# Moving the deferred token tiles' share of the last evacuations of a spectral block into its inverse stage

## The chip, the cores and the metric

One NeuronCore of a Trainium2 chip runs the kernel. The metric is the device time of one execution in microseconds; lower is better. Before the change it is 485.93 (median of three runs, 485.89 to 487.13).

The engines' names: PE is TensorE (matrix products; PEld is its weight load), DVE is VectorE, ACT is ScalarE, POOL is GpSimd and SP is SyncE. Of these SP and POOL issue the transfers (DMA). Products are written to PSUM, eight banks, used here in four pairs; ACT and DVE copy ("evacuate") them to SBUF.

## The reference

The input `x` has 2048 tokens of 576 features. A spectral filter is added to it, and then a gated feed-forward network.

```python
def _A_ref(x, w_r, w_i):
    X = rfft2(x.astype(float32), axes=(-2, -1))
    X = X * (w_r + 1j * w_i)
    return irfft2(X, s=(S, D), axes=(-2, -1)).astype(bfloat16)

def _B_ref(x, w_gate, w_up, w_down):
    return (gelu(x @ w_gate) * (x @ w_up)) @ w_down

h = x + _A_ref(layernorm(x), w_r, w_i)
h2 = h + _B_ref(layernorm(h), w_gate, w_up, w_down)
```

## The kernel before

The Fourier transforms are products with constant tables. The 2048 tokens stand as 16 tiles of 128 (tile c holds every sixteenth token). There are five parts in time:

1. Layer norm and the first transform over the tokens (to about 20 us), in the order of the list `SEQ1`.
2. The spectral stages over 16 groups of frequencies (20 to 43 us), in the order of the list `SEQF`. `D`/`d` and `B` finish the forward transform, `T` multiplies by the filter, `V`/`v` begin the way back, `R`/`r` do so for the 32 remainder columns that do not fit into 256, four groups at a time. Capital and small letter are the two halves of one accumulation on PE; behind the small one stand its evacuations.
3. The inverse stage (43 to 55 us), in the order of the list `SEQ`, for token tiles 0 to 7. `I`/`i` (function `i_mm`, line 837) are the products over groups, `E` their evacuation to GS, `N`/`o` (`n_mm`, line 854) the products with the inverse table IT, `a` (line 860) adds the result to x on DVE; then `s`, `q`, `c`, `n`, `u`, `e` normalise the tile and transpose it. `G0` and `G1` are the first products of the network.
4. The network's products with the gate and up weights (line 946), and among them the inverse stage of token tiles 8 to 15, which are *deferred* (`def_i`, line 996, and `def_n`, line 1013).
5. The products with the down weights (line 1046 and 1058) and the output, by blocks of 512 tokens.

The order on each engine is that of the lists: each engine runs its instructions in the order in which the program issues them. A recorder (`Prog`) turns reads and writes of named tiles into semaphore waits. An instruction that must wait for more than a few semaphores is preceded by wait instructions of their own, issued at line 307.

What the change touches:

- `st_V` writes group i's result to the tile V, `[128, 2, 2, 16 token tiles, 16 groups, 2, 4]`, in one or two evacuations (line 608, in `ev`). For the last one, V15, ACT and DVE take 256 elements per partition each. All token tiles are in them.
- `st_R` handles the remainder. For its first three sets (R0 to R2) one evacuation goes to the buffer RB, and eight transfers of 8 KB carry it to the places in VR. They are split by `k = (2 * j + t_) % 3 > 0`: three on SP, five on POOL. For the last set, R3, eight evacuations of 32 partitions by 128 elements go to VR directly, four on ACT and four on DVE.
- `i_mm(c, False)` makes four products from V (*main* products); `i_mm(c, True)` makes four more and then two from VR. VR is read with the token tile as its innermost index.
- `LOADS` says behind which step the transfers of tables and of the first weights are issued on SP. `"r0": "t"` calls `tab_load` behind r0: it waits for the last copy of the filter, and issues the tables VT (parts 2 to 5), DT, IT and IDT. The pieces a0 to a5 and b0 to b5 are the network's first weights (256 and 896 columns wide); each waits until PE has come to the step by which it is named.
- `SLOT` gives each `I`, `N` and `u` a pair of PSUM banks: the free one that was used longest ago. R3 has pair 3 (banks 6 and 7) and V15 pair 2 (banks 4 and 5). In `SEQ`, I0, I1 and I2 take pairs 0, 1 and 2, and N0 pair 3.

Of the kernel before, what the change touches and what calls it, by code (L numbers as in the profile page):

```python
# [12 lines left out]
NZ, NY = 5, 3  # L13
# [16 lines left out]
DENG, BENG = ['act', 'dve', 'act', 'act', 'act', 'act', 'act', 'act', 'dve', 'act', 'act', 'act', 'act', 'act', 'act', 'act'], ['act', 'dve', 'act', 'act', 'act', 'act', 'act', 'dve', 'act', 'act', 'act', 'act', 'act', 'act', 'act', 'act']  # L30
LOADS = {"r0": "t", ".I0": "a0 a1 a2 a3 a4 a5", ".N0": "b0", ".i3": "b1", ".o1": "b2", ".N3": "b3", ".o3": "b4 b5", ".i7": "d"}
RENG = ['dve', 'act', 'act', 'act', 'act']
QR = ((0, 1), (1, 2), (2, 3), (3, 4), (4, 8), (8, 16))
DEF0, DSTEP = 3, 4
SEQ = """I0 I1 I2 i0 E0S i1 E1S i2 E2A N0 I3 o0 i3 N1 I4 o1 a0 E3S N2 o2 a1 s0A q0 i4 a2 s1A I7 c0 N3 E4S q1 s2D i7 I6 o3 E7A i6 c1 N4 o4 a3 q2 E6A c2 N7 I5 o7 a4 n0P N6 s3A a7 i5 n1P n2P q3 c3 o6 u1 U1 u2 E5A u0 U2 a6 n3P e1A e2D U0 N5 u3 e0A o5 a5 U3 G0 e3D G1""".split()

# [10 lines left out]
def build_tables():  # L47
# [106 lines left out]
    assert np.allclose(VN[0, 0], VN[0, 1])  # L154
    T["VTAB"] = np.stack([v if k else v.reshape(128, 4, 16, 4).transpose(0, 1, 3, 2).reshape(128, 256) for v, k in ((VN[0, 0], 1), (VN[0, 0], 0), (VN[1, 0], 1), (VN[1, 1], 1), (VN[1, 0], 0), (VN[1, 1], 0))], 1).reshape(128, -1)

# [175 lines left out]
def _build(nc, A_x, A_w_r, A_w_i, B_w_gate, B_w_up, B_w_down, out):  # L332
# [78 lines left out]
    TR = sb.alloc("TR", [128, 2, 2, 2, 128], BF16)  # L411
    RB = sb.alloc("RB", [128, 3, 2, 2, 4, NT], BF16)

# [18 lines left out]
    P.op(POOL, lambda g: g.memset(EXQ[:, :], -0.5), w=["EXQ"])  # L432
    P.op(POOL, lambda g: g.memset(VR[:, :, :, :, :], 0.0), w=[("V", g, 2 + t) for g in range(NG) for t in range(2)])
    xv = A_x[0].rearrange("(p c) d -> p c d", c=NT)
# [243 lines left out]
    def st_V(i, second, engs):  # L678
        g, z, b0 = GORD[i], i % NZ, FB["V", i]

        def mm(h, o, ct, first, last, after):
            c, t_ = ct
            return P.op(PE, lambda t: t.matmul(bank(b0 + o, 0, 128, 128 * c, 128 * c + 128), TP[64 * h:64 * h + 64, z, o, t_, c:256:2], VT[64 * h:64 * h + 64, 0 if g else 2 + o, t_, :],  # L683
                                               start=first, stop=last), r=[("T", z), "VT" if g else "VT2"], w=[("PS", b0 + o)], after=after)

        halves(("V", i), second, [[(c, t_) for c in range(2) for t_ in range(2)]] * 2, mm)
        if not second:
            return
        v5 = V[:, :, :, :, g, :, :].rearrange("p c t n j e -> p j (c t n) e")
        n = 2 // len(engs)  # L690
        for a, e in enumerate(engs):
            ev(e, v5[:, n * a:n * a + n], banks(b0 + a, n, 256).rearrange("p a (c e) -> p a c e", e=4), [("PS", b0 + a + k) for k in range(n)], [("V", g, a + k) for k in range(n)])

    def st_R(q, second):
        js = range(4 * q, 4 * q + 4)
        b0 = FB["R", q]

        def mm(h, o, pt, first, last, after):
            part, t_ = pt
            return P.op(PE, lambda t: t.matmul(bank(b0 + o, 0, 128, 128 * part, 128 * part + 128), TR[64 * h:64 * h + 64, q % 2, o, t_, :], VT[64 * h:64 * h + 64, 4 + o if part else 1, t_, :], start=first, stop=last),  # L700
                        r=[("TR", q % 2, j) for j in range(4)] + ["VT2" if part else "VT1"], w=[("PS", b0 + o)], after=after)

        halves(("R", q), second, [[(part, t_) for part in range(1 + (q == 3)) for t_ in range(2)]] * 2, mm)
        if not second:
            return
        keys = [("PS", b0), ("PS", b0 + 1)]
        if q < 3:
            ev(RENG[q], RB[:, q, :, :, :, :].rearrange("p t o e n -> p o t (e n)"), banks(b0, 2, 128).rearrange("p o (t x) -> p o t x", t=2), keys, [("RB", q)])
            for j, i in enumerate(js):
                for t_ in range(2):  # L710
                    k = (2 * j + t_) % 3 > 0
                    P.dma((SP, POOL)[k], VR[64 * t_ + 32 * (j % 2):64 * t_ + 32 * (j % 2) + 32, GORD[i], :, :, :], RB[32 * j:32 * j + 32, q, t_, :, :, :], f"r{q}{k:d}", r=[("RB", q)], w=[("V", GORD[i], 2 + t_)])
            return
        for i in js:
            j, g = i % 4, GORD[i]
            for t_ in range(2):
                dst = VR[64 * t_ + 32 * (j % 2):64 * t_ + 32 * (j % 2) + 32, g, :, :, :].rearrange("p o e n -> p o (e n)")
                src = PS[32 * j:32 * j + 32, b0 * 512:(b0 + 2) * 512].rearrange("p (a c) -> p a c", a=2)[:, :, 128 * (i == LAST) + 64 * t_:128 * (i == LAST) + 64 * t_ + 64]
                ev((ACT, DVE, DVE, ACT)[j], dst, src, keys, [("V", g, 2 + t_)])

# [35 lines left out]
    def tab_load():  # L756
        P.op(SP, None, after=[last])
        P.dma(SP, VT[:, 2:6, :, :].rearrange("p a b c -> p (a b c)"), dram["VTAB"][:, 512:1536], "vt2", w=["VT2"])
        P.dma(SP, DT[:, :, :].rearrange("p a b -> p (a b)"), dram["DTAB"][:, :], "dt", w=["DT"])
        P.dma(SP, IT[:, :, :, :].rearrange("p a b c -> p (a b c)"), dram["ITAB"][:, :], "it", w=["IT"])  # L760
        P.dma(SP, IDT[:, :], dram["EYE"][:, :], "eye", w=["IDT"])

# [14 lines left out]
    def loads(w):  # L777
        for v in LOADS.get(w, "").split():
            if v in "td":
                (tab_load if v == "t" else tab2_load)()  # L780
            else:
                wg0_part(int(v[1]), *((0, 256, ["WGA"]) if v[0] == "a" else (256, 1152, [("WG", 0, i) for i in range(4)])))
# [24 lines left out]
    vk = [vmain, vmain, vtail]  # L807
    vkeys = vmain + vtail


    SLOT, last, held, ing = {}, [sorted(used.values()).index(used[2 * b]) - 4 for b in range(4)], set(), False
    for t, w in enumerate(SEQ):
# [18 lines left out]
    def i_mm(c, second):  # L831
        b, e = SLOT["I", c], ends.setdefault(("I", c), [None, None])
        for j in range(2 + second):
            for r in range(2):
                o, r0 = r ^ (not second), 64 * r
                lhs = V[r0:r0 + 64, j, o, c, :, :, :] if j < 2 else VR[r0:r0 + 64, :, :, :, c].rearrange("p g o e -> p (g o e)")
                e[o] = P.op(PE, lambda t, r0=r0, o=o, j=j, lhs=lhs: t.matmul(bank(b + o, 0, 128, 0, KW), lhs, DT[r0:r0 + 64, 2 * o + j if j < 2 else 4, 0:KW], start=(not second and j == 0), stop=(second and j == 2)),  # L837
                            r=vk[j] + ["DT"], w=[("PS", b + o)], after=[e[o]] if second and j == 0 else [])
# [119 lines left out]
    def gu_first(i):  # L958
        for a in range(4):
# [4 lines left out]
           "s": lambda c, e: sq(c, ENG[e]), "q": ln2_q, "c": ln2_c, "n": lambda c, e: norm(c, ENG[e]), "u": lambda c: turn_mm(c, False), "U": lambda c: turn_mm(c, True),  # L964
           "e": turn_ev, "G": gu_first}
    for w in SEQ:
# [16 lines left out]

    fdead = ["DT", "IT", "J0", "J1", "ZD"] + [(n_, c) for n_ in ("ATB", "ATS") for c in range(NT)] + [("G", i // 2, i % 2) for i in range(10)] + [*[("Y", a) for a in range(NY)], *[("RB", a) for a in range(3)]]
    fdead += [("T", a) for a in range(NZ)] + [("TR", a, j) for a in range(2) for j in range(4)]
# [3 lines left out]
    def def_i(c, second):  # L989
        e = ends.setdefault(("X", c), [None, None])  # L990
        for j in range(3):
            for r in range(2):
                o, r0 = r ^ (not second), 64 * r
                t_ = j if j < 2 else r
                lhs, rhs = (V[r0:r0 + 64, o, t_, c, :, :, :], DP[r0:r0 + 64, 2 * o + t_, :]) if j < 2 else (VR[r0:r0 + 64, :, :, :, c].rearrange("p g o e -> p (g o e)"), DP[r0:r0 + 64, 4 + o, :])
                e[o] = P.op(PE, lambda t, o=o, t_=t_, lhs=lhs, rhs=rhs, j=j: t.matmul(bank(6 + o, 0, 128, HK * t_, HK * t_ + HK), lhs, rhs, start=(not second and j == 0), stop=(second and j == 2)),  # L996
                            r=vk[o if j < 2 else 2] + ["DP"], w=[("PS", 6 + o)], after=[e[o]] if second and j == 0 else [])
        if not second:
# [133 lines left out]
```

## Time and profile before

| what | value |
|---|---|
| median of the runs | 485.93 us (485.89, 485.93, 487.13) |
| the profiled execution's own time | 485.97 us |
| its span in the trace | 484.2 us |
| granted TensorE clock | 1.00 |
| L946 (gate and up), products of one shape | 2142 + 486, 373 to 376 ns each |
| L1046 (down) | 2160, 283 ns each |
| L837 + L854 (inverse stage), share of the last chain | 0.7% + 0.2% |

The span is what the trace covers; the time of an execution has 1.8 us around it. PE has 99% of the span as busy time, since products overlap and each counts from its start to its modelled end, so the share does not tell where it waits. For that one reads the chain of work that ended last and the timeline. A line of the timeline has the start, the length, the engine and source line, the operation, the tiles written and read, the shape and the number of instructions merged; in brackets stands the engine's idle time before them and who ended it. "SPq" lines are issues of transfers, and their length is that of the issue, not of the transfer.

### The profile page before, as it was taken

To read this page: it belongs to the slowest core of one execution; us is meant where nothing else is said; L and a number is where in the kernel's file an instruction comes from. 1 tells how busy PE (TensorE), PEld (TensorE's weight loads), DVE (VectorE), ACT (ScalarE), POOL (GpSimd) and SP (SyncE) were. 2 spreads that over 40 slices of the span, in tenths; PEclk is the share of its full clock that TensorE was granted. 3 is DMA by queue.
4 is the path that set the end of the run, shared out by engine and by line. 5 is a ranking of instruction groups with operands and counts; after the bars stand their busy time and mean duration, and the time that the engine had idled before them with its cause. 6 is when DMAs were issued, how large, how long until landed. Compare 5 with 4: busy or idle time off the path is not lost.

```text
span 484.2 us, 12895 instructions
## 1 busy us (share of the span) xinstructions
PE 477.5 (99%) x5875; PEld 304.4 (63%) x5876; DVE 183.3 (38%) x366; ACT 146.3 (30%) x295; POOL 52.2 (11%) x88
## 2 busy tenths in 40 slices
PE   8999999999999999999999999999999999999998
PEld 4877765555588744444688644444788544445884
DVE  7898755665500144333200234333101233333011
ACT  6998753434300032233100132223100133223000
POOL 6873317010120000000000000000000000000000
DMA  8865889941430001000000011000000000000000
GB/s 283 215 142 160 251 279 282 374 109 27 173 100 27 26 15 23 20 1 0 3 14 15 26 24 23 13 1 1 3 14 27 14 1 1 0 1 1 3 26 26
DMA packets 28582, 33.19 MB, mean 69 GB/s; under 512 B 12640, under 2 KB 21872, under 8 KB 28528
## 3 DMA queue, kind: packets, MB, share of 16 engines
q1 hardware_dynamic: 24864, 19.87, 14.3%
q0 software_dynamic: 3664, 12.50, 8.1%
q8 instruction: 46, 0.75, 0.7%
q14 instruction: 8, 0.07, 0.1%
HBM read 26.21 MB, written 2.36 MB: 59 GB/s over the span
## 4 chain that ended last, share of the span: by engine, by line
PE 95%; DMA 1%; DVE 1%; POOL 1%; SPq 0%; issue 0%; POOLq 0%; DVEq 0%
PE PS L946 58%; PE PS L1046 27%; PE PS L642 2%; PE PS L1058 2%; PE PS L683 2%; DMA XO<-in_A_x_dram 1%; PE PS L553 1%; PE PS L662 1%; PE PS L837 1%; PE PS L996 1%; DVE XO L860 1%; SPq L242 0%; PE PS L1013 0%; PE PS L854 0%; POOL XN L569 0%
## 5 line engine op out<-in xcount | busy, mean ns | idle before, releaser
L946 PE MATMUL PS<-HT,WG 64*128 64x512 bf16 (+1 forms) x2142 | 233.5, 373 | 0.1
L946 PEld LDWEIGHTS PS<-HT,WG 64*128 64x128 bf16 x2142 | 116.1, 94 | 104.4 <-DVE AT L955 0.2
L954 ACT ACTIVATE GL<-PS 128x512 bf16<-128x512 f32 x144 | 85.7, 596 | 281.7 <-PE PS L946 281.7
L955 DVE TENSOR_TENSOR AT<-GL,PS 128x512 bf16<-128x512 bf16 x144 | 98.8, 687 | 166.0 <-ACT GL L954 166.0
L1046 PE MATMUL PS<-WD,AT 64*128 64x288 bf16 x2160 | 133.0, 283 | 0.0
L1046 PEld LDWEIGHTS PS<-WD,AT 64*128 64x128 bf16 x2160 | 114.3, 94 | 18.7
L1033 DVE TENSOR_TENSOR OS<-PS,XO 128x288 bf16<-128x288 f32 (+2 forms) x32 | 13.2, 452 | 125.5 <-PE PS L1046 118.0
L946 PE MATMUL PS<-HT,WGX 64*128 64x512 bf16 x486 | 53.5, 376 | 0.0
L946 PEld LDWEIGHTS PS<-HT,WGX 64*128 64x128 bf16 x486 | 25.7, 94 | 26.7
L863 ACT ACTIVATE OS<-XO,NM 128x576 bf16<-128x576 bf16 x15 | 11.6, 773 | 11.4 <-DVE XO L1017 11.4
L642 PE MATMUL PS<-FT,U 64*128 64x288 bf16 x160 | 13.3, 283 | 0.0
L675 DVE TENSOR_TENSOR TP<-YS,WS 128x1024 bf16<-128x1024 bf16 x16 | 11.0, 686 | 0.4 <-PE PS L683 0.2
L564 ACT ACTIVATE U<-PS 128x384 bf16<-128x384 f32 (+2 forms) x31 | 10.5, 427 | 1.2 <-PE PS L553 1.1
L496 DVE BATCH_NORM_STATS2 ST<-XO 128x6 f32<-128x288 bf16 x26 | 10.0, 441 | 1.8 <-DMA XO<-in_A_x_dram 1.8
L242 POOL DMA_DIRECT2D WG<-in_B_w_gate_dram x9 | 6.1, 679 | 35.5 <-DMA WG<-in_B_w_gate_dram 32.1
L683 PE MATMUL PS<-VT,TP 64*128 64x128 bf16 x256 | 9.9, 217 | 0.0
L553 PE MATMUL PS<-ATS,XO 128*128 128x128 bf16 x96 | 8.2, 220 | 1.5 <-POOL ATS L522 0.8
L242 POOL DMA_DIRECT2D WD<-in_B_w_down_dram x9 | 6.7, 756 | 22.9 <-PE PS L1013 22.9
L608 ACT ACTIVATE CUS<-PS 128x576 bf16<-128x576 f32 x14 | 9.1, 656 | 0.4 <-PE PS L642 0.2
L1058 PE MATMUL PS<-WD,AT 128*128 128x448 bf16 (+1 forms) x72 | 9.0, 286 | 0.0
L538 PE MATMUL PS<-ZD 128*128 128x512 bf16 x23 | 7.5, 484 | 1.5 <-POOL ZD L431 1.5
L608 ACT ACTIVATE YS<-PS 128x576 bf16<-128x576 f32 x14 | 8.8, 653 | 0.1
(88 smaller groups left out, 231.3 us busy)
## 6 DMA issues: line engine op xcount, KB each, us to landing
WD<-in_B_w_down_dram POOLq DMA_DIRECT2D x9, 576.0 KB, 13.0
WG<-in_B_w_up_dram SPq DMA_DIRECT2D x6, 576.0 KB, 6.6
WG<-in_B_w_gate_dram POOLq DMA_DIRECT2D x6, 576.0 KB, 6.2
out_dram<-OS SPq DMA_DIRECT2D x30, 72.0 KB, 1.7
XO<-in_A_x_dram SPq DMA_DIRECT2D x3, 576.0 KB, 7.1
WGX<-in_B_w_up_dram SPq DMA_DIRECT2D x2, 576.0 KB, 4.5
WGX<-in_B_w_gate_dram POOLq DMA_DIRECT2D x2, 576.0 KB, 5.8
HT<-HN SPq DMA_TRANSPOSE x60, 2.4
```

The source lines that it names most:

```text
L242: fn = lambda e: e.dma_start(out_ap, in_ap)
L553: P.op(PE, lambda t, b=b, lhs=lhs, p0=p0, p1=p1, s=s, e=e, o=o, c=c: t.matmul(bank(b, p0, p1, o, o + 128), lhs, ATS[:, c, :], start=s, sto ...
L608: fn = (lambda v: v.tensor_copy(dst, src)) if eng == DVE else (lambda a: a.activation(dst, src, ACTF.Copy))
L642: return P.op(PE, lambda t: t.matmul(bank(b0 + o, 0, 128, 0, 2 * HK), U[64 * h:64 * h + 64, us, 2 * i:2 * i + 2, :, :], FT[64 * h:64 * h + ...
L683: return P.op(PE, lambda t: t.matmul(bank(b0 + o, 0, 128, 128 * c, 128 * c + 128), TP[64 * h:64 * h + 64, z, o, t_, c:256:2], VT[64 * h:64 ...
L863: P.op(ACT, lambda a, c=c, out=out: a.activation(out, XO[:, c, 0:D], ACTF.Square, bias=NM[:, c:c + 1], accum_out=SB2[:, 1, c:c + 1]), r=[( ...
L946: op = P.op(PE, lambda t, h0=h0, kt=kt, wt=wt, b=b, s=(not second and j == 0), e=(second and j == n - 1): t.matmul(bank(b, 0, 128, c0, c1) ...
L954: P.op(ACT, lambda a: a.activation(GL[:, s2, :], bank(b0), ACTF.Gelu_apprx_tanh), r=[("PS", b0)], w=[("GL", s2)])
L955: P.op(DVE, lambda v: v.tensor_tensor(AT[:, f, :], GL[:, s2, :], bank(b0 + 1), op=ALU.mult), r=[("GL", s2), ("PS", b0 + 1)], w=[("AT", f)])
L1033: P.op(DVE, lambda v: v.tensor_tensor(OS[:, p % 2, d0:d1], bank(b, 0, 128, 0, d1 - d0), XO[:, c, d0:d1], op=ALU.add), r=[("PS", b), ("X", ...
L1046: e[h] = P.op(PE, lambda t, f=f, h=h, r0=r0, j=j: t.matmul(bank(b0 + h, 0, 128, 0, 288), AT[r0:r0 + 64, f, 128 * p:128 * p + 128], WD[r0:r ...
L1058: P.op(PE, lambda t, b=b, d0=d0, d1=d1, f=f, j=j: t.matmul(bank(b, 0, 128, 0, d1 - d0), AT[:, f, 128 * p:128 * p + 128], WD[:, f, d0:d1], ...
```

## The change

There are four parts.

- **Halves by token tile.** V15's evacuation is cut in two by token tile (`v_half`): tiles 0 to 7 behind v15, as before; tiles 8 to 15 at a new step `l15` in `SEQ`. R3's eight evacuations to VR carry tiles 0 to 7 only; tiles 8 to 15 go at a new step `l3` (`tail_late`): two evacuations on ACT to RB (96 and 32 partitions), and from there eight transfers of 4 KB to VR, four on SP and four on POOL. The layout of VR, RB and one table is changed so that the halves are contiguous. `def_i` waits for the late parts.
- **The order of `SEQ`.** It began `I0 I1 I2 i0 E0S i1 E1S i2 E2A N0`; now it begins `I0 I1 i0 l15 E0S I2 i1 E1S i2 E2A l3 N0`. Pairs 2 and 3 are held until l15 and l3. I0, I1, I2 and N0 get the same pairs as before.
- **Four per queue.** The transfers of R0 to R2 are split by `k = t_ ^ (j % 2)`: four on SP, four on POOL. Each now carries two runs of 128 bytes per partition instead of one of 256.
- **Tables.** `tab_load` is called behind r1 instead of r0, without IT; IT is issued behind r2's transfers.

On SP the order was: r0's three transfers, VT, DT, IT, IDT, r1's three, r2's three, a0 to a5, b0 and on. Now it is: r0's four, r1's four, VT, DT, IDT, r2's four, IT, a0 to a5, l3's four, b0 and on. The number of products and their shapes on PE are the same.

```diff
-LOADS = {"r0": "t", ".I0": "a0 a1 a2 a3 a4 a5", ".N0": "b0", ...
+LOADS = {"r1": "t", "r2": "i", ".I0": "a0 a1 a2 a3 a4 a5", ".N0": "b0", ...
-SEQ = """I0 I1 I2 i0 E0S i1 E1S i2 E2A N0 I3 o0 i3 ...
+SEQ = """I0 I1 i0 l15 E0S I2 i1 E1S i2 E2A l3 N0 I3 o0 i3 ...
...
-    VR = sb.alloc("VR", [128, NG, 2, 4, NT], BF16)
+    VR = sb.alloc("VR", [128, 2, NG, 2, 4, NT // 2], BF16)
...
-    RB = sb.alloc("RB", [128, 3, 2, 2, 4, NT], BF16)
+    RB = sb.alloc("RB", [128, 3, 2, 2, 2, 32], BF16)
...
     def st_V(i, second, engs):
...
+        if i == LAST:
+            v_half(i, 0, ("V", g))
+            return
...
+    def v_half(i, k, key):
+        for a, e in enumerate((ACT, DVE)):
+            src = bank(FB["V", i] + a, 0, 128, 0, 256).rearrange("p (q x) -> p q x", q=4)[:, :, 32 * k:32 * k + 32].rearrange("p q (n e) -> p q n e", e=4)
+            ev(e, V[:, :, :, 8 * k:8 * k + 8, GORD[i], a, :].rearrange("p c t n e -> p (c t) n e"), src, [("PS", FB["V", i] + a)], [(*key, a)])
...
     def st_R(q, second):
...
-                    k = (2 * j + t_) % 3 > 0
-                    P.dma((SP, POOL)[k], VR[64 * t_ + 32 * (j % 2):64 * t_ + 32 * (j % 2) + 32, GORD[i], :, :, :], RB[32 * j:32 * j + 32, q, t_, :, :, :], ...
+                    k = t_ ^ (j % 2)
+                    P.dma((SP, POOL)[k], tail_place(i, t_, slice(0, 2)), RB[32 * j:32 * j + 32, q, t_, :, :, :].rearrange("p k o x -> p k (o x)"), ...
...
-                src = PS[...][:, :, 128 * (i == LAST) + 64 * t_:128 * (i == LAST) + 64 * t_ + 64]
+                src = PS[...][:, :, 128 * (i == LAST) + 64 * t_:128 * (i == LAST) + 64 * t_ + 32]
...
+    def tail_late(q, engs):
+        b0 = FB["R", 3]
+        for p0, p1, c, e in ((0, 96, 0, engs[0]), (96, 128, 128, engs[1])):
+            ev(ENG[e], RB[p0:p1, 0, :, 1, :, :].rearrange("p t o x -> p o t x"), PS[p0:p1, ...][:, :, :, 32:64],
+               [("PS", b0), ("PS", b0 + 1)], [("RB", 0, p0)])
+        for i in range(12, 16):
+            for t_ in range(2):
+                j = i % 4
+                P.dma((SP, POOL)[t_], tail_place(i, t_, 1), RB[32 * j:32 * j + 32, 0, t_, 1, :, :].rearrange("p o x -> p (o x)"), f"rl{t_}", ...
...
     def tab_load():
...
-        P.dma(SP, IT[:, :, :, :].rearrange("p a b c -> p (a b c)"), dram["ITAB"][:, :], "it", w=["IT"])
         P.dma(SP, IDT[:, :], dram["EYE"][:, :], "eye", w=["IDT"])
+
+    def it_load():
+        P.dma(SP, IT[:, :, :, :].rearrange("p a b c -> p (a b c)"), dram["ITAB"][:, :], "it", w=["IT"])
...
-    SLOT, last, held, ing = {}, [...], set(), False
+    SLOT, last, held, ing = {}, [...], {FB["R", 3] // 2, FB["V", LAST] // 2}, False
...
+        elif k == "l":
+            held.discard(FB["R" if i == 3 else "V", i] // 2)
...
-                            r=vk[o if j < 2 else 2] + ["DP"], w=[("PS", 6 + o)], ...
+                            r=(vk[o] if j < 2 else vtail) + vlate + ["DP"], w=[("PS", 6 + o)], ...
...
+           ... "l": lambda q: tail_late(q, "AA") if q == 3 else v_half(q, 1, ("VM", GORD[q]))}
```

More of the change, by code (lines that the diff above doesn't have):

```diff
@@ L34 @@
 DEF0, DSTEP = 3, 4
-SEQ = """I0 I1 I2 i0 E0S i1 E1S i2 E2A N0 I3 o0 i3 N1 I4 o1 a0 E3S N2 o2 a1 s0A q0 i4 a2 s1A I7 c0 N3 E4S q1 s2D i7 I6 o3 E7A i6 c1 N4 o4 a3 q2 E6A c2 N7 I5 o7 a4 n0P N6 s3A a7 i5 n1P n2P q3 c3 o6 u1 U1 u2 E5A u0 U2 a6 n3P e1A e2D U0 N5 u3 e0A o5 a5 U3 G0 e3D G1""".split()
+SEQ = """I0 I1 i0 l15 E0S I2 i1 E1S i2 E2A l3 N0 I3 o0 i3 N1 I4 o1 a0 E3S N2 o2 a1 s0A q0 i4 a2 s1A I7 c0 N3 E4S q1 s2D i7 I6 o3 E7A i6 c1 N4 o4 a3 q2 E6A c2 N7 I5 o7 a4 n0P N6 s3A a7 i5 n1P n2P q3 c3 o6 u1 U1 u2 E5A u0 U2 a6 n3P e1A e2D U0 N5 u3 e0A o5 a5 U3 G0 e3D G1""".split()
 def _np_bf16(a):
@@ L154, in build_tables @@
     assert np.allclose(VN[0, 0], VN[0, 1])
[L155 removed]
+    T["VTAB"] = np.stack([v if k else v.reshape(128, 4, 2, 8, 4).transpose(0, 1, 2, 4, 3).reshape(128, 256) for v, k in ((VN[0, 0], 1), (VN[0, 0], 0), (VN[1, 0], 1), (VN[1, 1], 1), (VN[1, 0], 0), (VN[1, 1], 0))], 1).reshape(128, -1)
     kr = np.arange(1, K2)
@@ L432, in _build @@
     P.op(POOL, lambda g: g.memset(EXQ[:, :], -0.5), w=["EXQ"])
-    P.op(POOL, lambda g: g.memset(VR[:, :, :, :, :], 0.0), w=[("V", g, 2 + t) for g in range(NG) for t in range(2)])
+    P.op(POOL, lambda g: g.memset(VR[:, :, :, :, :, :], 0.0), w=[(k, g, 2 + t) for k in ("V", "VL") for g in range(NG) for t in range(2)])
     xv = A_x[0].rearrange("(p c) d -> p c d", c=NT)
@@ L807, in _build @@
     vk = [vmain, vmain, vtail]
-    vkeys = vmain + vtail
-    SLOT, last, held, ing = {}, [sorted(used.values()).index(used[2 * b]) - 4 for b in range(4)], set(), False
+    vlate = [("VM", GORD[LAST], a) for a in range(2)] + [("VL", GORD[i], 2 + t) for i in range(12, NG) for t in range(2)]
+    vkeys = vmain + vtail + vlate
+    SLOT, last, held, ing = {}, [sorted(used.values()).index(used[2 * b]) - 4 for b in range(4)], {FB["R", 3] // 2, FB["V", LAST] // 2}, False
     for t, w in enumerate(SEQ):
@@ L981, in _build @@
         wd_load(j)
-    fdead = ["DT", "IT", "J0", "J1", "ZD"] + [(n_, c) for n_ in ("ATB", "ATS") for c in range(NT)] + [("G", i // 2, i % 2) for i in range(10)] + [*[("Y", a) for a in range(NY)], *[("RB", a) for a in range(3)]]
+    fdead = ["DT", "IT", "J0", "J1", "ZD"] + [(n_, c) for n_ in ("ATB", "ATS") for c in range(NT)] + [("G", i // 2, i % 2) for i in range(10)] + [*[("Y", a) for a in range(NY)], *[("RB", a) for a in range(3)], ("RB", 0, 0), ("RB", 0, 96)]
     fdead += [("T", a) for a in range(NZ)] + [("TR", a, j) for a in range(2) for j in range(4)]
```

31 lines of the change are left out of this document (18 added, 13 removed).

## The prediction

> **What bounds the kernel now.** I read the page first (busy shares, the chain that ended last), then the timeline where the spectral part hands over to its inverse stage, then single issues and their landings. On the page TensorE is busy for 99% of the span and holds 95% of the last chain, at a granted clock of 1.00 in every stretch I asked for.
>
> ```profile
> PE 477.5 (99%) x5875; PEld 304.4 (63%) x5876; DVE 183.3 (38%) x366; ACT 146.3 (30%) x295; POOL 52.2 (11%) x88
> PE 95%; DMA 1%; DVE 1%; POOL 1%; SPq 0%; issue 0%; POOLq 0%; DVEq 0%
> ```
>
> The change lies in the few microseconds where that chain leaves PE. The chain in order of time (start, length, what):
>
> ```profile
> 43.06 0.42 DVE V L608
> 43.48 0.14 issue
> 43.62 1.16 PE PS L837 x16
> 44.77 0.33 issue
> 45.10 1.08 PE PS L837 x14
> 46.18 0.30 PE PS L854 x4
> ...
> 47.01 0.76 DVE XO L860
> 47.76 0.37 DVE GS L843
> 48.13 1.47 DVE XO L860 x2
> ```
>
> PE waits for the last V evacuation, runs 16 main products (I0, I1, I2 and the first four of i0), waits again ahead of i0's VR products, runs on to N0, and from 47.01 VectorE leads until PE takes over for good at 55.4. So what counts is when N0 starts (46.06): a0 on VectorE waits for o0 behind it, and VectorE is then busy 93 to 100% of every microsecond up to 55. A delay of N0 is a delay of the end, one for one; a gain there as well. The timeline of the same place:
>
> ```profile
> 43.36 1.09 ACT L608 ACTIVATE VR<-PS 32x128 bf16<-32x128 f32 x4
> 43.50 1.19 DVE L608 CAST VR<-PS 32x128 bf16<-32x128 f32 x4
> 45.10 0.34 PE L837 MATMUL PS<-DT,VR 64*128 64x288 bf16 x2 [0.33 <-issue]
> 46.06 0.42 PE L854 MATMUL PS<-GS,IT 64*128 64x288 bf16 x4
> 46.22 0.65 ACT L608 ACTIVATE GS<-PS 128x576 bf16<-128x576 f32 x1
> 47.01 0.76 DVE L860 TENSOR_TENSOR XO<-PS,XO 128x576 bf16<-128x576 f32 x1 [0.73 <-PE PS L854]
> ```
>
> Who ends the second wait? VectorE's evacuations end at 44.69, but the last remainder copy on SP, issued at 41.04, landed 3.6 later, at 44.64:
>
> ```profile
> 41.04 1.53 SPq L242 DMA_DIRECT2D VR<-RB  x1
> VR<-RB SPq DMA_DIRECT2D x1, 8.0 KB, 3.6
> ```
>
> Line 307 has four semaphore waits on PE's load queue between 44.67 and 45.05, 0.107 apart, and the first waits for this copy's semaphore: landing 44.64, first wait 44.67, product 45.10. So this release is the copy's landing plus 0.46.
>
> **The change, part by part.**
>
> *First halves.* VectorE's part of v15 falls from 256 to 128 elements per partition: 0.42 becomes 0.29 (the 32x128 CASTs on line 608 take 0.286, and length goes with elements). I0 starts at 43.05 + 0.29 + 0.15 (the old step from 43.47 to 43.62) = 43.49, 0.13 earlier. The eight VR evacuations fall to 64 elements: on VectorE 0.286 − 64 × 1.05 ns = 0.22, the slope being (0.423 − 0.286)/128; on ACT about 0.21. VectorE ends its four at 43.36 + 4 × 0.234 = 44.30 instead of 44.69.
>
> *Order.* I2 now comes after i0, since its bank pair holds V15 until l15. Only 12 main products, six pairs 0.122 apart, stand ahead of the VR products: PE is free for them at 44.22.
>
> *Remainder copies, four per queue.* SP is no longer held by the table loads for r1; for r2 it starts when ACT has evacuated RB, at 39.81 as now. Four issues at the present step of 0.60 to 0.63 put the last at 41.67. Landing after issue: 2.0 (POOL's copies of the same group) to 3.6 (SP's last now, behind the inverse table). With that table gone from ahead of them I take 2.4, the slowest of POOL's: 44.07, and VR products at 44.07 + 0.46 = 44.53. Ends for the range: 43.7 and 45.3. Each copy now has 64 pieces of 128 bytes instead of 32 of 256; no row here shows that, and the same ends hold it. The table loads that move to r1 start behind four SP issues, at about 37.5 instead of 36.13; VT must be there for V15 at 42.3 (lands 2.7 after issue, 40.2) and DT at 43.5 (3.4, 41.3): covered by two microseconds.
>
> *l15.* VectorE's second half ends at 44.30 + 0.30 = 44.60, and I2 may start at 44.75. Then I2, i1 and i2, eight pairs × 0.122: PE reaches N0 at 45.73 instead of 46.06. So far a gain of 0.33.
>
> *l3.* Here it turns. The two RB evacuations stand on ACT behind E2A, and N0 takes the bank pair that R3 held, so N0 waits for the second of them; before, N0 waited for its GS tile and the table alone. E2A starts 0.16 after PE reaches N0 (46.22 against 46.06), and E1S on ACT leaves no earlier place: 45.95. It takes 0.65, to 46.60. Two evacuations of 128 elements at 0.27 each (the 32x128 ACT rows: 264 ns) end at 47.14, and N0 starts 0.15 later: 47.29. Against 46.06 that is **+1.23** (1.13 to 1.35 with 0.25 to 0.30 for each and E2A up to 0.06 earlier). Behind it stand I3, o0 and i3 on PE, hence a0 and VectorE's whole run.
>
> *The inverse table behind the copies.* It is issued at about 42.3 and lands by 46.1 if it takes the 3.8 of the first 448 KB weight piece, 47.5 with its own 5.2 of now. N0's new wait until 47.14 mostly hides it; without that cover it would cost 0.4 to 1.8 of its own.
>
> *Eight late copies.* POOL has nothing until n0P at 49.8: free. On SP they stand behind a5 (ends 47.1) and ahead of b0: 4 × 0.63 = 2.5, so b0 goes out at 49.6 instead of 47.27, and with it b1 to b5. Their semaphore is needed by the first 512-column products of line 946 at 59.4; the last piece lands at 52.14 + 6.5 = 58.6, which leaves 0.8. The issue of b0, the landing of the last piece, and the last 256-column products ahead of the first 512-column ones (a look at 59.38 to 59.44 answers with these six, one at 59.4 to 59.5 with both widths):
>
> ```profile
> 47.27 0.59 SPq L242 DMA_DIRECT2D WG<-in_B_w_gate_dram  x1
> WG<-in_B_w_up_dram SPq DMA_DIRECT2D x1, 112.0 KB, 6.5
> 59.18 0.61 PE L946 MATMUL PS<-HT,WG 64*128 64x256 bf16 x6
> ```
>
> In the new kernel they are needed at 59.4 + 1.23 = 60.6 and land 1.7 (b0 lands faster on an empty queue: a0 took 2.3) to 2.3 later, at 60.3 to 60.9. Stall 0 to 0.3; I take 0.2.
>
> *Deferred tiles.* Their first product (61.6) now also waits for the late copies, which land by 53: nothing.
>
> **Sum.** The profiled run took 485.97 (span 484.2, 1.8 around it), 0.04 above the median of 485.93. 485.97 + 1.23 + 0.20 = **487.4**. Nothing later gives it back: PE runs without a gap from 55.5.
>
> **Rivals.**
>
> A. *The remainder lands late.* A fourth copy on SP with today's 3.6 lands at 45.27; VR products 45.73, eight pairs from 45.88, N0 reached at 46.86, E2A 47.02 to 47.67, evacuations to 48.21, N0 48.36, +2.30: 488.5. For it: landings on SP have been 2.7, 3.2 and 3.6, rising with each copy. Against: the table ahead of them is gone. The Trainium skill (DMA: Bandwidth & Descriptors, Issuing engines are not separate DMA queues) has it that spreading issues over engines saves only the issue time, usually small beside the DMA; by it the new split brings nothing by itself and the last landing just moves with its issue, which is this rival. The trace agrees only in part: here issue is not small, four take 2.5.
>
> B. *The gap closes and the rest hides (not slower).* If the late evacuations were done before PE reaches N0, or VectorE had slack after it, N0 would start at 45.73 (46.15 if the table sets it): 485.6 to 486.1. For it: ACT is idle for 1.03 before E0S and 0.53 after E2A. Against: ACT keeps its order, E2A cannot start before i2 ends, and l3 is behind it; it decides only if l3 ends by 46.0 rather than 47.14. The Trainium skill (Perfetto Trace Analysis, Optimizing Scalar/DVE Operations) says that where these engines are not saturated but cause bubbles elsewhere, breaking instructions up may finish work sooner; ACT and VectorE are idle here, so the rule would give this rival. It holds for the first halves; it does not speak of the second half's place.
>
> C. *The first weights come late.* Two of nine SP copies out of RB took 2.30 and 1.53 to issue instead of 0.59. One such among the four late ones adds 1.7: last piece at 62.3 against 60.6, +1.65: 485.97 + 1.23 + 1.65 = 488.9.
>
> D. *The inverse table sets N0.* With SP's last copy again at 1.53 the table goes out at 43.2 and lands at 48.4: N0 48.55, +2.5: 488.7 with the 0.2.
>
> **Chances.** Forecast 0.60, its own range 487.0 to 488.2; A 0.14, B 0.09, C 0.12, D 0.05. About 0.3% (1.46 us) is what a measurement of this kernel can tell from no change; the line is 487.39, and the forecast sits on it. Half of it is slower: 0.30 + 0.14 + 0.12 + 0.05 = 0.61, less 0.03 for mild forms of these: 0.58. Faster by 0.3% would need 484.5, more than all PE idle time between 42.6 and 46.1: 0.02. Within: 0.40. The range from 486.6 to 489.0 leaves out B and the far ends of C and D.
>
> **What would show it.** I0 at 43.5; VR products near 44.5 with the wait before them at 0.3 or less; N0 (line 881) near 47.3 with PE idle for some 1.4 before it, released by ACT's second RB evacuation; a0 near 48.25; first 512-wide products near 60.8. It is wrong if N0 starts before 46.5, if a DMA releases N0, or if a later N0 does not move a0.

## The result, and the profile after

The changed kernel takes 488.53 us (median of 10 runs, 487.18 to 490.24), against 486.37 (median of 10, 485.89 to 487.13) for the kernel before, run beside it: a ratio of 1.0043, with a 95% interval of 1.0028 to 1.0057. It is slower by 2.16 us. The forecast of 487.4 lay 1.1 below the measured time and the range from 486.6 to 489.0 holds it.

The profiled execution of the changed kernel took 489.48, near the upper end of its runs; its span is 487.7, the granted clock 1.00. The part ahead of the inverse stage was 1.1 longer in it as well: VectorE's evacuation of V15 begins at 44.16 instead of 43.06. Most of that is one wait of PE, 0.78 until 29.19, for a piece of the table VT that landed at 29.14; before, it landed at 27.82. The same kernel, profiled again (e12 below), had that piece at 27.88 and V15 at 43.19, and in the other kernels V15 begins anywhere from 43.10 to 43.95. So all places below are counted from that evacuation ("V15"), which takes such differences out.

The busy shares and the chain that ended last, on the page of the changed kernel:

```profile
PE 478.0 (98%) x5875; PEld 311.8 (64%) x5876; DVE 182.8 (37%) x367; ACT 146.8 (30%) x298; POOL 53.3 (11%) x89
PE 88%; SPq 5%; DMA 3%; DVE 1%; ACT 1%; issue 1%; DVEq 0%
```

PE's busy time grew by 0.5 only, and its count is the same: no work was added to it. What changed is that the chain, followed back from the end, now leaves PE twice, for transfers. The same chain in order of time, from the hand-over to the network's products (start, length, what):

```profile
42.84 1.18 SPq L242
44.03 0.04 issue
44.07 3.85 DMA IT<-c_itab
47.92 0.92 issue
48.84 0.42 PE PS L881 x4
...
49.78 0.76 DVE XO L887
...
55.65 7.34 DMA WG<-in_B_w_up_dram
62.98 0.04 issue
63.03 1.04 PE PS L973 x7
```

Two waits stand in it: one ahead of N0 (line 881, at 48.84), where the chain names the inverse table, and one ahead of the first 512-column products at 63.03, whose weights landed at 62.98. The first label deserves doubt: 0.92 us of "issue" lie between the table's landing and N0. The timeline of the place shows what fills them:

```profile
44.16 0.29 DVE L608 CAST V<-PS 128x128 bf16<-128x128 f32 x1 [0.19 <-PE PS L683]
44.49 0.92 DVE L608 CAST VR<-PS 32x64 bf16<-32x64 f32 x4
44.60 0.91 PE L864 MATMUL PS<-DT,V 64*128 64x288 bf16 x12 [0.25 <-ACT V L608]
46.27 0.34 PE L864 MATMUL PS<-DT,VR 64*128 64x288 bf16 x2 [0.76 <-DMA VR<-RB]
47.63 0.65 ACT L608 ACTIVATE GS<-PS 128x576 bf16<-128x576 f32 x1
48.18 0.56 ACT L608 ACTIVATE RB<-PS 96x128 bf16<-96x128 f32 x2
48.84 0.42 PE L881 MATMUL PS<-GS,IT 64*128 64x288 bf16 x4 [1.24 <-DMA IT<-c_itab]
49.78 0.76 DVE L887 TENSOR_TENSOR XO<-PS,XO 128x576 bf16<-128x576 f32 x1 [2.09 <-PE PS L881]
```

The evacuations to RB on ACT end at 48.74, and N0 starts 0.10 later; the table had been there for 0.8. One more view tells the same: the semaphore waits of line 307 on PE's load queue, with the shortest, median and longest in ns.

```profile
L307 PEldq EVENT_SEMAPHORE  x5: 51/51/1662, 45.8 to 47.1; - x5
```

Four of them took 51 ns and belong to the remainder copies; the fifth began at 47.12 and held PE for 1.66, to 48.78. VectorE, which was idle for 0.73 ahead of a0 before, is now idle for 2.09 there.

### The profile page after: what moved, and what is told of

The parts are those of the page before. It is cut to its first block, busy times and chain, and to the rows that moved or that the text cites. A ratio compares the mean times of both kernels' runs of the same rounds, so it can differ in the third digit from the quotient of the medians.

```text
span 487.7 us, 12908 instructions
## 1 busy us (share of the span) xinstructions
PE 478.0 (98%) x5875; PEld 311.8 (64%) x5876; DVE 182.8 (37%) x367; ACT 146.8 (30%) x298; POOL 53.3 (11%) x89
## 4 chain that ended last, share of the span: by engine, by line
PE 88%; SPq 5%; DMA 3%; DVE 1%; ACT 1%; issue 1%; DVEq 0%
PE PS L973 57%; PE PS L1073 27%; SPq L242 5%; PE PS L1085 2%; DMA WG<-in_B_w_up_dram 2%; DMA IT<-c_itab 1%; DMA VT<-c_vtab 1%; PE PS L1023 1%; DVE XO L887 1%; PE PS L642 1%; ACT YS L608 1%; PE PS L683 0%; PE PS L1040 0%; ACT CUS L608 0%; DVE OS L947 0%
## 5 line engine op out<-in xcount | busy, mean ns | idle before, releaser
L973 PEld LDWEIGHTS PS<-HT,WG 64*128 64x128 bf16 x2142 | 117.3, 94 | 103.7 <-DMA WG<-in_B_w_up_dram 0.9
L1073 PEld LDWEIGHTS PS<-WD,AT 64*128 64x128 bf16 x2160 | 119.6, 94 | 13.4
L1060 DVE TENSOR_TENSOR OS<-PS,XO 128x288 bf16<-128x288 f32 (+2 forms) x32 | 13.2, 452 | 125.5 <-PE PS L1073 118.0
L973 PEld LDWEIGHTS PS<-HT,WGX 64*128 64x128 bf16 x486 | 26.9, 94 | 25.6
L242 POOL DMA_DIRECT2D VR<-RB x16 | 8.3, 533 | 9.6 <-ACT RB L608 9.6
```

Source lines behind the costliest of these rows:

```text
L242: fn = lambda e: e.dma_start(out_ap, in_ap)
L973: op = P.op(PE, lambda t, h0=h0, kt=kt, wt=wt, b=b, s=(not second and j == 0), e=(second and j == n - 1): t.matmul(bank(b, 0, 128, c0, c1) ...
L1060: P.op(DVE, lambda v: v.tensor_tensor(OS[:, p % 2, d0:d1], bank(b, 0, 128, 0, d1 - d0), XO[:, c, d0:d1], op=ALU.add), r=[("PS", b), ("X", ...
L1073: e[h] = P.op(PE, lambda t, f=f, h=h, r0=r0, j=j: t.matmul(bank(b0 + h, 0, 128, 0, 288), AT[r0:r0 + 64, f, 128 * p:128 * p + 128], WD[r0:r ...
```

## The experiments

Each kernel differs from the changed kernel by the edit shown, unless it says "from the kernel before". Times are medians, with the kernel before as it ran in the same batch (486.33, 486.41 and 486.40 in the three). Each batch ran on a chip of its own, so the ratios, and not the times, compare kernels of different batches (e1 to e4, e5 to e9, e10 to e12). The table has the places in each profiled run, in us from V15: the VR products, N0, G0, the first 512-column products, and the end of the span. One profile is one execution: that of e10 is the slowest of its 11 runs (487.25), that of e12 the fastest of its 5 (487.53).

| kernel | VR | N0 | G0 | 512 | end | time | ratio to before |
|---|---|---|---|---|---|---|---|
| before | 2.05 | 3.01 | 12.43 | 16.35 | 441.13 | | |
| after | 2.11 | 4.67 | 14.09 | 18.87 | 443.52 | 488.53 | 1.0043 [1.0028, 1.0057] |
| e1_bank | 2.00 | 3.63 | 13.88 | 18.32 | 442.97 | 488.06 | 1.0033 [1.0021, 1.0045] |
| e2_copies_late | 1.59 | 4.16 | 13.58 | 17.51 | 442.23 | 487.63 | 1.0028 [1.0017, 1.0038] |
| e3_both | 2.05 | 3.65 | 13.90 | 17.83 | 442.56 | 487.83 | 1.0033 [1.0021, 1.0046] |
| e4_tables_back | 1.72 | 4.28 | 13.70 | 18.20 | 442.86 | 488.60 | 1.0041 [1.0028, 1.0054] |
| e5_halves_only | 1.62 | 2.75 | 12.64 | 16.57 | 441.28 | 486.96 | 1.001 [1.000, 1.002] |
| e6_tables_alone | 1.80 | 3.87 | 13.29 | 17.22 | 441.98 | 486.98 | 1.001 [0.9999, 1.002] |
| e7_one_sem | 1.79 | 2.75 | 12.16 | 16.43 | 441.11 | 486.56 | 1.000 [0.9991, 1.001] |
| e9_both_pairs | 2.10 | 3.87 | 13.67 | 17.60 | 442.32 | 487.47 | 1.0018 [1.0009, 1.0027] |
| e10_halves_pairs | 2.23 | 3.36 | 12.87 | 16.79 | 441.51 | 486.64 | 1.000 [0.999, 1.0011] |
| e11_pairs_one_sem | 2.12 | 3.26 | 12.77 | 16.70 | 441.42 | 486.08 | 0.9994 [0.9985, 1.0003] |
| e12_changed_again | 1.91 | 4.47 | 13.89 | 17.89 | 442.54 | 488.13 | 1.0038 [1.0024, 1.0051] |

Where PE does not wait for weights, the first 512-column products stand 3.92 or 3.93 behind G0 in the table; what is above that is a delay by the weights (0.85 in the changed kernel's profile, in which PE's idle time of 0.67 is counted from a modelled end).

Three theories of the loss are used in the expectations. BANK: N0 waits for ACT's late evacuations, since they read the pair of banks that it takes. TABLE: the inverse table, issued later, sets N0. QUEUE: the four late copies on SP hold back the network's first weights.

### e1_bank: l3 behind N1

N0 and l3 change places, with I3 to N1 between; b0 and b1 still come behind the late copies.

```diff
-LOADS = {... ".N0": "b0", ".i3": "b1", ...
+LOADS = {... ".l3": "b0 b1", ...
-SEQ = """... i2 E2A l3 N0 I3 o0 i3 N1 I4 ...
+SEQ = """... i2 E2A N0 I3 o0 i3 N1 l3 I4 ...
```

> The changed kernel with l3 moved behind N1, so that N0 takes bank pair 0 and not R3's; the first weights b0 and b1 stay behind the late copies on SP. In the changed kernel's profile V15's evacuation on VectorE starts at 44.17, N0 at 48.84, the inverse table landed at 47.92. Theory BANK (N0 waits for ACT's second late evacuation): N0 comes 0.8 to 0.9 earlier counted from V15's evacuation, 3.8 to 3.9 behind it, now released by the table or by PE's own arrival; the first weights land when they did, so the wait for them grows from 0.7 to about 1.5 and the total changes by less than 0.3. Theory TABLE (the table, issued behind the copies, sets N0): N0 stays 4.6 to 4.7 behind V15's evacuation.

N0 came 1.63 behind the VR products instead of 2.56, so BANK holds for 0.9 of the wait. In the timeline of e1_bank the rest is the table's: it landed at 3.58 after V15, N0 followed at 3.63, and here the named releaser is right. The wait for weights did not grow to 1.5, as expected, but fell to 0.33.

```profile
45.11 0.35 PE L864 MATMUL PS<-DT,VR 64*128 64x288 bf16 x2 [0.66 <-DVE V L608]
46.73 0.42 PE L881 MATMUL PS<-GS,IT 64*128 64x288 bf16 x4 [0.30 <-DMA IT<-c_itab]
56.99 1.71 PE L973 MATMUL PS<-HT,WG 64*128 64x256 bf16 x28 [0.89 <-DVE XO L887]
61.43 0.82 PE L973 MATMUL PS<-HT,WG 64*128 64x512 bf16 x6 [0.33 <-DMA WG<-in_B_w_up_dram]
```

The gain did not reach the end. With pair 3 held until behind N1, the rule for `SLOT` gives the later steps other pairs; a5 then reads the pair that G0 writes, and G0 waited 0.89 for it. That was not expected, and it gave back most of what N0 had gained: N0 is 1.04 sooner than in the changed kernel, G0 0.21.

### e2_copies_late: SP's late copies behind the weights

```diff
-LOADS = {... ".o3": "b4 b5", ...
+LOADS = {... ".o3": "b4 b5 k", ...
...
+            elif v == "k":
+                late_copies(0)
```

The function `late_copies(0)` issues SP's four; POOL's four stay at l3.

> The changed kernel with the four late copies on SP issued behind the last first-weight piece (b5) instead of ahead of b0; POOL's four stay. Theory QUEUE (the copies hold back the weights): the wait of 0.67 ahead of the first 512-column products goes, N0 stays where it was, the total falls by 0.5 to 0.9 against the changed kernel. Rival (the weights are limited by what the DMA engines move): the wait stays above 0.4.

The last weights landed at 15.12 after V15, and PE went on to the 512-column products at 17.51 without a wait: the late copies do hold the weights back, by 2.7 to 3.7 against the two profiles of the changed kernel (17.84 and 18.82). So QUEUE is right for the 0.67 of the first of them; in the second, e12, there was next to nothing to gain. N0 stayed 2.57 behind the VR products with the same idle time of 1.24, so this edit leaves BANK alone.

### e3_both: e1 and e2 together

> Both edits: l3 behind N1, and SP's late copies behind b5. BANK and QUEUE: N0 3.8 to 3.9 behind V15's evacuation, no wait for weights above 0.1, total 1.3 to 1.7 below the changed kernel, 0.4 to 0.9 above the kernel before. TABLE: N0 unchanged, total only 0.5 to 0.9 below the changed kernel.

N0 at 3.65, no wait for weights (landed at 15.86), but the wait of 0.89 ahead of G0 is there again, so the time of 487.83 shows no gain over e2 that can be told from nothing. The forecast of 1.3 to 1.7 below the changed kernel is missed: by the ratios it is 0.5. With e1 and e2 it says: the two causes are separate, and a third, made by e1's own edit, hides what the first is worth.

### e4_tables_back: tables and split as before, l3 ahead of N0

```diff
-LOADS = {"r1": "t", "r2": "i", ...
+LOADS = {"r0": "t", ...
-                    k = t_ ^ (j % 2)
+                    k = (2 * j + t_) % 3 > 0
...
+        it_load()
```

> The changed kernel with the remainder copies split and the tables issued as in the kernel before (three on SP, five on POOL; all tables behind r0); halves, l15 and l3 stay. BANK: N0 still waits for the second late evacuation, 4.6 to 4.8 behind V15's evacuation; total within 0.4 of the changed kernel. TABLE: the table lands before PE gets there, N0 comes to 3.1 to 3.4 behind V15's evacuation, total 1.0 to 1.5 lower.

This is the cleanest test of TABLE. The table landed 1.20 ahead of V15, and still N0 came 2.56 behind the VR products. From the timeline of e4_tables_back:

```profile
45.52 0.34 PE L865 MATMUL PS<-DT,VR 64*128 64x288 bf16 x2 [0.37 <-DVE V L608]
48.09 0.42 PE L882 MATMUL PS<-GS,IT 64*128 64x288 bf16 x4 [1.24 <-issue]
```

The same idle time of 1.24 as in the changed kernel, now with no transfer to name. While l3 stands ahead of N0, the table's place costs nothing. The ratio of 1.0041 is that of the changed kernel.

### e5_halves_only: halves, without l3 ahead of N0 and with the tables back

From e3, with e4's edit, and three steps given their pairs by hand so that G0 need not wait:

```diff
-            b = min((b for b in range(2 * ing, 4) if b not in held), key=lambda b: last[b])
+            b = {"N7": 0, "I5": 1, "N6": 2}.get(w, min((b for b in range(2 * ing, 4) if b not in held), key=lambda b: last[b]))
```

> The halves alone, placed so that nothing waits for them: l3 behind N1 and N0 in pair 0, with N7, I5 and N6 put into pairs 0, 1 and 2 so that G0 finds the pairs that it had (in the runs before, G0 waited 0.89 for a5's pair); SP's late copies behind b5; remainder split and tables as in the kernel before. Counted from V15's evacuation on VectorE, in the kernel before: VR products +2.05, N0 +3.01, G0 +12.43. BANK and QUEUE account for all of the loss: VR products +1.6 to +2.1 (they follow the last remainder copy's landing by 0.35 to 0.46, which the halves do not move), N0 1.1 to 1.2 behind them, G0 +12.2 to +12.6, no wait for weights; total within 0.4 of the kernel before, so the halves gain almost nothing. Rival (splitting evacuations costs by itself): total 0.5 or more above the kernel before.

N0 came at 2.75, 0.26 sooner than before the change. But G0 came 0.21 later than before, since the pairs given by hand made a wait of their own, for ACT's evacuation out of the pair that N7 was given (timeline of e5_halves_only):

```profile
52.32 0.42 PE L886 MATMUL PS<-GS,IT 64*128 64x288 bf16 x4 [0.58 <-ACT GS L608]
```

The time is 0.55 above the kernel before, which by its size is the sign that was set for the rival (0.5 or more); but that wait is a cause of its own, so the time does not tell what the halves alone are worth, and e10 asks again.

### e6_tables_alone: tables and split, nothing else

From the kernel before, with the changed kernel's `LOADS` for r1 and r2, its split of four per queue, and `it_load`:

```diff
-LOADS = {"r0": "t", ...
+LOADS = {"r1": "t", "r2": "i", ...
-                    k = (2 * j + t_) % 3 > 0
+                    k = t_ ^ (j % 2)
```

> The kernel before with only the copies four per queue, the tables behind r1 and the inverse table behind r2's copies. Theory TABLE HIDDEN (the table's late landing is a second limit that the wait for l3 covered): it lands 3.5 to 3.8 behind V15's evacuation, N0 starts 0.05 later instead of at +3.01, total 0.6 to 0.8 above the kernel before. Rival (the table costs nothing): N0 +3.0, total within 0.2.

Here nothing covers the table, and it sets N0 (timeline of e6_tables_alone):

```profile
46.30 0.33 PE L839 MATMUL PS<-DT,VR 64*128 64x288 bf16 x2
47.61 0.42 PE L856 MATMUL PS<-GS,IT 64*128 64x288 bf16 x4 [0.98 <-DMA IT<-c_itab]
```

N0 is 0.86 later than before, and the end 0.85 later. By the medians it is 0.57, with an interval that touches 1. So the table's new place has a price which the wait for l3 hides in the changed kernel.

### e7_one_sem: fewer semaphores for the remainder

From the kernel before. PE's wait for the remainder is a chain of four wait instructions (44.67 to 45.05 before the change), each for one or two semaphores; here the sets share theirs, and two are left.

```diff
-                    P.dma(..., f"r{q}{k:d}", ...
+                    P.dma(..., f"r{k:d}", ...
```

> The kernel before with one semaphore per queue for the remainder copies of all sets instead of one per set and queue, so that i0's VR products wait for four semaphores instead of eight. Theory CHAIN OF WAITS (the wait instructions on PE, 0.107 apart, add to the landing): VR products follow the last landing by 0.15 to 0.25 instead of 0.46, N0 +2.75 to +2.85, total 0.2 to 0.3 lower. Rival (they overlap with the wait itself): landing to product stays 0.4 or more.

```profile
45.15 0.35 PE L837 MATMUL PS<-DT,VR 64*128 64x288 bf16 x2
59.80 0.39 PE L946 MATMUL PS<-HT,WG 64*128 64x512 bf16 x2 [0.16 <-DMA WG<-in_B_w_up_dram]
```

The VR products followed the main products without a wait, since the last copy had landed at 1.11, so the theory is not tested here; e11 asks again. N0 was 0.26 and G0 0.27 sooner, and yet the end is where it was (441.11 and 441.13) and the time is unchanged: the weights landed at 16.39, and the 512-column products came 4.27 behind G0 instead of 3.92. So in this profile a second limit took the whole of a gain at N0. As an improvement it is a miss.

### e9_both_pairs: e3 with the pairs given by hand

> The changed kernel (its tables and its split of the remainder copies) with l3 behind N1, SP's late copies behind b5 and the pairs as in the halves-alone kernel. The inverse table then sets N0: +3.6 to +3.8 behind V15's evacuation, G0 +13.0 to +13.2, no wait at G0 and none for weights; total 0.5 to 0.8 above the kernel before and 1.5 below the changed one.

G0 no longer waits for a5, and the ratio is 1.0018 instead of 1.0038 for the changed kernel, run again in e12; the intervals overlap by a hair. It was to be 0.5 to 0.8 above the kernel before, and is 1.06. N0 is the table's again, at 3.87, and the wait of e5 (0.57 here, at N7) came with the pairs, so G0 stands at 13.67 and not at 13.0 to 13.2:

```profile
47.72 0.42 PE L885 MATMUL PS<-GS,IT 64*128 64x288 bf16 x4 [0.45 <-DMA IT<-c_itab]
53.85 0.42 PE L885 MATMUL PS<-GS,IT 64*128 64x288 bf16 x4 [0.57 <-ACT GS L608]
```

### e10_halves_pairs: halves alone, with G0 starting on another pair

From e3 with e4's edit; `SLOT` as it falls, and the first products of the network take pairs 1, 2, 0 instead of 0, 1, 2.

```diff
-            assert not held & {0, 1}
+            assert not held & {1, 2}
...
-        return 2 * (m % 3 if m < 36 else m % 4)
+        return 2 * ((m + 1) % 3 if m < 36 else m % 4)
```

> The halves alone as before (l3 behind N1, SP's late copies behind b5, tables and remainder split as in the kernel before), but with the pairs left to the rule and the network's first products turned by one pair (its first one in pair 1, its second in pair 2), since a5 still holds pair 0. In the halves-alone kernel N0 came 0.26 earlier than in the kernel before, but PE then waited 0.58 for ACT's evacuation of I6, whose pair N7 had been given. Theory (that wait came from the forced pairs): it is gone, G0 +12.1 to +12.3 behind V15's evacuation (before: +12.43), total 0.1 to 0.4 below the kernel before. Rival (the late halves on ACT and VectorE cost it): G0 stays at +12.5 or more, total not below the kernel before.

Now the halves stand without a new wait of more than 0.1 for banks, table or weights, and the time is that of before: 486.64 and 486.40, 1.000 [0.999, 1.0011]. What holds the VR products is the remainder (timeline of e10_halves_pairs):

```profile
44.38 0.91 PE L869 MATMUL PS<-DT,V 64*128 64x288 bf16 x12 [0.25 <-ACT V L608]
46.17 0.34 PE L869 MATMUL PS<-DT,VR 64*128 64x288 bf16 x2 [0.88 <-DMA VR<-RB]
```

PE had its main products done 0.88 earlier; the last copy on SP landed 1.77 after V15, and the product followed 0.46 later.

The wait of e5 is gone, as the theory had it, but the gain that it promised did not come: G0 stands at 12.87 and not at 12.1 to 12.3, and the time is not below that of before, which are the signs set for the rival. Its cause, the late halves on ACT and VectorE, is not what the profile shows, though. G0 is 0.44 later than before: 0.18 is the later remainder, 0.17 is the new order, and 0.09 comes behind N0, where I3 begins (47.63) just after VectorE has evacuated i1 (47.59). As to the order: N0 stands 1.13 behind the VR products instead of 0.96, because I2's main products, which used to run while PE waited for the remainder, now come behind that wait. In e5 and e11, where PE does not wait ahead of N0 either, it is 1.13 and 1.14; in e7, with the old order, 0.96.

### e11_pairs_one_sem: e10 and e7 together

> The same with one semaphore per queue for the remainder copies. CHAIN OF WAITS: VR products +1.4 to +1.6 instead of +1.6 to +2.1, with no wait ahead of them above 0.2; G0 +12.0 to +12.2; total 0.3 to 0.6 below the kernel before. Rival (evacuations set the VR products by now): no change against the kernel with turned pairs.

The product followed the last landing by 0.09 instead of 0.46; but in this run the last copy landed at 2.03, and the VR products came at 2.12 and not at 1.4 to 1.6:

```profile
45.58 0.35 PE L869 MATMUL PS<-DT,VR 64*128 64x288 bf16 x2 [0.78 <-DMA VR<-RB]
```

What counts is how many wait instructions stand behind the one that waits longest. In e10 the last landing is SP's, which the first of four waits for; in e4 and e5 it is POOL's, which the second waits for, and the product follows 0.35 later; here the last of two waits for it. G0, at 12.77, missed its 12.0 to 12.2.

486.08 is the lowest median of all, 0.32 below the kernel before; the interval of the ratio, 0.9985 to 1.0003, does not exclude that it equals the kernel before. No version clearly beats that one.

### e12_changed_again: the changed kernel, unchanged

> The changed kernel once more, beside these on one chip. N0 4.1 to 4.7 behind V15's evacuation, 2.5 to 2.6 behind the first VR products; 0.3 to 0.8 of waiting for the first weights; V15's evacuation itself between 43.0 and 44.2, which no edit here moves; total 1.8 to 2.5 above the kernel before.

488.13 against 486.40, +1.73: the loss is there again, a little below the 1.8 to 2.5 that were expected. e10, in the same batch on the same chip, has none: its interval (0.999 to 1.0011) lies below that of the changed kernel (1.0024 to 1.0051). In the profile the chain names the table once more, and ACT's evacuation ends just ahead of N0. First the chain, then the timeline:

```profile
42.88 3.74 DMA IT<-c_itab
46.62 1.04 issue
47.66 0.42 PE PS L881 x4
```

```profile
46.46 0.65 ACT L608 ACTIVATE GS<-PS 128x576 bf16<-128x576 f32 x1
47.00 0.56 ACT L608 ACTIVATE RB<-PS 96x128 bf16<-96x128 f32 x2
47.66 0.42 PE L881 MATMUL PS<-GS,IT 64*128 64x288 bf16 x4 [1.24 <-issue]
```

The table landed 1.04 ahead of N0 and the last evacuation to RB ended 0.10 ahead of it. The weights landed at 17.84 and were used at 17.89, 4.00 behind G0, so at most 0.07 was lost to them in this run; 0.3 to 0.8 had been expected.

## Why the prediction was right, and where its sizes were off

Its terms, in us from V15, beside the two profiles of the changed kernel:

| step | predicted | after | e12 |
|---|---|---|---|
| I0 | 0.44 | 0.44 | 0.44 |
| last remainder copy lands | 1.02 | 1.65 | 1.45 |
| VR products | 1.48 | 2.11 | 1.91 |
| second RB evacuation ends | 4.09 | 4.58 | 4.37 |
| N0 | 4.24 | 4.67 | 4.47 |
| N0 against before | +1.23 | +1.66 | +1.46 |
| inverse table lands | 3.05 to 4.45 | 3.75 | 3.43 |
| b0 issued | 6.55 | 7.75 | 7.55 |
| last weights land | 17.25 to 17.85 | 18.82 | 17.84 |
| delay by them (512 behind G0, less 3.93) | 0.2 | 0.85 | 0.07 |

*l3 ahead of N0: right.* PE stood idle for 1.24 ahead of N0, behind ACT's second late evacuation, and did so in all four profiles with l3 ahead of N0 (both of the changed kernel, e2 and e4); e4 took the table out of the question, and e1 took this wait away by moving l3 (the 0.30 that is left is the table's), as did e3, e9 and e10 among other edits. A delay of N0 is a delay of the end, as the prediction had it: a0 is 0.95 behind N0 in both profiles and before, and in e12 N0 is 1.46 later and the end 1.41. "A gain there as well" did not hold: in e5 and e7 N0 was 0.26 sooner, and a wait for a bank in the one and for weights in the other left nothing of it.

*First halves: right in themselves.* The evacuation of V15 took 0.29, VectorE's four to VR 0.92 (0.94 predicted), and I0 stands at 0.44. In e10 the time is that of before all the same, because the VR products go by the last remainder copy, and the new order then costs 0.17 at N0. So of the gain of 0.33 that the prediction puts ahead of l3 nothing is left when the remainder lands late. In e5, where it landed at 1.27, N0 was 0.26 sooner; but so it was in e7, without the halves and with a landing at 1.11. The Trainium skill's rule on breaking instructions up (Perfetto Trace Analysis, Optimizing Scalar/DVE Operations) agrees with the first halves: the work they feed, I0, began 0.13 sooner. It says only that work may be completed sooner; in e10 the end came no sooner.

*The remainder: the step that failed.* "With that table gone from ahead of them I take 2.4" put the last landing at 1.02; it was 1.45 to 1.65. The last issue began as predicted (1.32 ahead of V15, against 41.67, which is 1.38 ahead), but it was a long one again, 1.18 and 0.97 instead of 0.60, and its copy took 2.97 and 2.77 from there to land, though the table was no longer ahead. Less the excess of the issue over 0.60, that is 2.39 and 2.40, and 2.39 in e1 and e3 as well, where the last issue took 1.08 and 1.12. So the 2.4 fits an ordinary issue, and what the sum left out is the long one. It had stood in the profile before (1.53 and 2.30 among nine), and the prediction names it in rivals C and D alone; A's 3.6 holds it unnamed. No run here changes that issue by itself, so this rests on the rows. It makes +0.43 to +0.63 on the VR products; some 0.20 of it came back on the way to N0: E2A began 1.36 behind the VR products instead of 1.42, its end and the RB evacuations took 1.11 together instead of 1.19, and N0 followed after 0.10 instead of 0.15. This is rival A's course of events, a late remainder, at a third to a half of its size at the VR products and a fifth to two fifths at N0 (A had them at 2.68 and 5.31); A's reason, landings that rise with each copy, does not hold by itself: in e2, e6, e9 and e10, where the long issue is not SP's last, the last copy took 1.8 to 2.1. That the measured 488.53 is A's 488.5 is thus a coincidence of sums. The split itself brought no landing that stands out: with four per queue the last copy landed at 1.14 to 1.65 (seven profiles), with three and five at 1.11 to 2.04 (six). The Trainium skill's rule that a second issuing engine saves only the time of issuing (DMA: Bandwidth & Descriptors, Issuing engines are not separate DMA queues) agrees so far; that this time is usually small does not fit here, as one issue took 0.60 of the 2.3 to 2.8 from issue to landing in e12, and the four in a row took 2.89 of SP's time.

*The table: right.* It is hidden under l3, and it was to cost 0.4 to 1.8 without that cover: it is 0.86 in e6's profile. Rival D's price was not reached, since the table went out 0.1 to 0.3 ahead of V15 and took 3.7 to 3.9.

*The late copies: too small.* Four were put at 2.5 and took 3.40 in both profiles, one of them 1.51; b0 went out 1.2 and 1.0 later than predicted. That is rival C in a mild form: the long issue added 0.9 and not 1.7, and most of it was taken up by the time that b1 to b5 would have waited anyway. In one profile the last piece also took 7.3 to land (6.4 in e12), and the 512-column products were 0.85 late; in e12 it was 0.07.

*The sum and its base.* +1.46 to +1.66 for N0 and 0.07 to 0.85 for the weights make +1.5 to +2.5; the ends of the two profiles, from V15, are 1.41 and 2.39 later, and the medians say +1.73 and +2.16; predicted was +1.43. The base was low too: the profiled 485.97 lies 0.40 below the median of the ten runs of the kernel before. That and the two sizes are the 1.1 between 487.4 and 488.53.

*Rival B* fell as argued: the late evacuations ended at 4.4 to 4.6 and not by 2.95. Where e1 and e3 moved l3 out of N0's way, the table held N0, and a wait for banks ahead of G0 followed; with both out of the way, e10 shows no gain.

What stays open: how much of the loss in time, and not in profiles, belongs to l3, to the weights and to the table. That they make it up together is shown by e10, which changes all three (and the pair that G0 starts on) and has no loss. The parts do not add up, since each covers another, and the differences between the variants are of the size of their intervals.

## What to carry to other kernels

Work that is put off must also be read out of something: look up who takes that bank or buffer next, and put the late read behind the first user that is on the path, not ahead of it. If an evacuation is to be cut so that the first half comes sooner, see first what its readers wait for last; here it was a transfer, the halves could not gain, and the products that were put behind the wait for their sake came later. When the chain names a transfer and a stretch of "issue" follows it, look for the engine that ends its work at the end of that stretch.

## What the runs showed of the hardware that was not expected

In all 13 profiles one of SP's issues of R2's copies takes 0.97 to 1.65 us instead of 0.60, and begins within 0.4 of the start of a 16 KB packet on the queue called "instruction". In the profile of the changed kernel that packet started at 42.67 and the issue of 1.18 at 42.84; before the change it was 41.03 and 41.04, the issue of 1.53 that the prediction shows. The one long issue among the late copies has such a packet too (50.16 and 50.36). The transfers of the changed kernel between 42.6 and 44.0 by queue (name, packets, MB, share):

```profile
q8 instruction: 1, 0.02, 4.3%
```

For R2's copies the two go together in every profile; that the one causes the other was not tried. Among the weight pieces there are long issues with no such packet beside them (1.75 at 51.98 in e7, whose packets there start at 48.25 and 56.90).

A chain of waits ahead of a product has a length of its own, and it matters which of them waits longest: 0.46 passed from the last landing to the product where the first of four waited for it (before, after, e10), 0.35 where it was the second (e4, e5), and 0.09 where it was the last of two (e11). The steps of the chain are 0.107 apart.
